# Attention scores with two heads in the two halves of the partitions, ahead of a mixture of experts

## The chip, the cores and the metric

The kernel runs on one core of one Trainium2 chip. The metric is the device time of one execution in microseconds (us); three executions of the kernel before took 622.19, 626.22 and 628.02 us, and their median, 626.22 us, is the time before.

## The reference

Attention over 4 batches of 8 heads, 768 positions, 64 dimensions per head. A query sees the first 4 keys (the sinks) and the 128 keys up to its own position. The result, 3072 tokens of 512 numbers, goes to a mixture of 8 experts that takes one expert per token.

```
scores = scale * np.matmul(q, k.transpose(0, 1, 3, 2))
keep = is_sink | in_window
a = np.exp(np.where(keep, scores, -1e9) - max); a = a / (sum + 1e-09)
x = np.matmul(a, v)                      # rows of 8 heads * 64
logits = xn @ en.T / tau;  expert_idx = argmax(logits)
out[mask] = gate_w[mask, None] * (relu(x[mask] @ w1[e]) @ w2[e])
```

## The kernel before

Everything runs on one core, in two stages: attention with routing, and then the eight experts one after the other. The change lies in the attention alone.

The attention works on 16 pairs of heads (`NP`), each pair in six blocks of 128 queries, in two groups of three blocks (`GROUPS`). For each block, TensorE (PE) computes the scores of both heads into one `sp` tile, which is two banks of PSUM, one per head, 260 columns each: the previous block's keys, the 4 sinks, the current block's keys (`scores`). VectorE (DVE) merges the two blocks by a mask (`merge`) and takes the maximum (`top`), ScalarE (ACT) the exponentials (`exp`). Per group, PE transposes the result, ACT copies it out of PSUM, GpSimd (POOL) cuts it into the parts that belong to each block of values (`sel`), PE multiplies these with the values (`av`) and with the experts' embeddings beside an identity (`xe`), and a DMA stores the rows (`xs<-xr`). There are three `sp` tiles and two further PSUM tiles `w`, which all the other products share.

Ahead of its scores, a pair's queries and keys are split into two parts of 12 bits each, so that fast products (float32r) reach float32 (`prep`). In the kernel before, the host lays every head out twice, in both halves of the 128 partitions. One head has its own loads of q and k (`qn`, `kn`, 128 partitions each) and its own split. The keys end up as `kt`, the first part in partitions 0 to 63 and the second part in 64 to 127: ACT rounds all 128 partitions (line 874), and POOL subtracts in the upper half (line 877). The queries are split by DVE into q1 (line 888) and q2 (line 892), each with the same numbers in both halves; for two heads of all, ACT makes q1. A score block of one head is then two products of 128 rows, q1 and q2 against `kt`, which adds up all four combinations of parts.

The first two pairs (`PLAIN`) are not split: their q and k lie in `raw1` and `raw2`, the staging buffers of the experts' weights, and are multiplied as float32, in one product of 128 rows per head, in which the keys of one head stand beside zeros for the other (line 914). Those buffers are loaded at the very start (`early_loads`, `plain_load`), by the queues of SyncE (SP) and ACT; DVE and POOL write the zeros.

The order on every engine is made ahead of time by a small planner (`Plan`): each piece of work has an engine, a planned duration and a key; among what can start, the smallest key goes first. `KEYS` holds the offsets of the keys by kind of work, `LAST` those of the last pair. Each engine then runs its list strictly in order.

Of the kernel before, what the change touches and what calls it, by code (L numbers as in the profile page):

```python
# [8 lines left out]
F32 = mybir.dt.float32  # L9
# [27 lines left out]
KEYS = dict(sel=-7, ps=1.25, pse=6.25, av=3.75, ote=-42.5, xe=4.25, xee=1.25, k1=7.5, k2=47.25, q1=9.75, q2=0.25, sc=16, mg=-0.25, tp=-0.5, ex=3.25, sk0=-72, sk1=23, tr=-0.75, te=-4.75, rt=2.25, vs=7.75, em=23.25, rc=5.75, lgm=-0.25)  # L37
LAST = dict(mg=9.25, xee=-16.75, tr=-28.25, sc=42.75, ex=31.25, k1=20, sel=7.75, av=35.25, ote=12.5, k2=67, sk1=63.5, rt=52.5, ps=14.75, xe=-2.5, tp=25, q1=25.5, pse=22.75, q2=-0.5, te=60.5, rc=8, lgm=-29.75, vs=63.75, sk0=-31.25, em=-27)
# [17 lines left out]
class Plan:  # L56
    """Orders tasks for engines that issue in order: among those that can start, the one with the smallest key."""
# [22 lines left out]
    def ready(self, t):  # L80
        """when what t waits for is there; None: not known yet"""
# [56 lines left out]
class Kernel:  # L138
# [5 lines left out]
    # ------------------------------------------------------------ constants  # L144
    def constants(self, cp):
# [7 lines left out]
        # run-time scalars: value = (hi + (lo < 0)) * 2^32 + lo, on all partitions  # L153
# [18 lines left out]
    def routing_tiles(self, cp):  # L172
# [17 lines left out]
        # integers on their way to float32  # L190
# [4 lines left out]
    def routing_constants(self):  # L195
        """two parts: GpSimd's, a store"""
        nc = self.nc

        def first():
            nc.gpsimd.memset(self.ones_b[:], 1.0)  # L200
            # tri[k, m] = 1 where k < m
            nc.gpsimd.affine_select(out=self.tri_b[:], in_=self.ones_b[:], pattern=[[1, P]], compare_op=ALU.is_gt, fill=0.0, base=0, channel_multiplier=-1)
            # 8 - e
            nc.gpsimd.iota(self.wi, pattern=[[0, NB], [-1, E]], base=E, channel_multiplier=0)
            # token index of (partition, block), and less NT
            nc.gpsimd.iota(self.tokid[:], pattern=[[P, B * NB]], base=0, channel_multiplier=1)
            nc.gpsimd.iota(self.i3, pattern=[[P, B * NB]], base=-NT, channel_multiplier=1)
            # the free axis, and the slots
# [1131 lines left out]
```

## Time and profile before

| | kernel before |
|---|---|
| median of 3 executions | 626.22 us |
| span of the profiled execution | 620.5 us |
| PE busy | 500.7 us, 81% |
| DVE busy | 367.5 us, 59% |
| ACT busy | 300.5 us, 48% |
| POOL busy | 284.8 us, 46% |
| DMA traffic | 87.45 MB, mean 141 GB/s |

The profile is one further execution with the hardware profiler on; its span runs from the first to the last instruction and leaves out what lies around it. Busy time counts an instruction from its start to its end; products overlap at their ends, so that a busy PE need not be at its peak. A share of the whole span is a mean over two stages that have little in common: the attention ends at about 243 us, and the experts fill the rest.

### The profile page before, as it was taken

Reading aid. Unit: us, or ns where it says so; the run is one execution under the profiler, and the core shown is the slowest. Engines: PE = TensorE matmul, PEld = TensorE weight load, DVE = VectorE, ACT = ScalarE, POOL = GpSimd, SP = SyncE. Lnnn points to the kernel's source line nnn. Section 1 sums busy time; section 2 is a strip of 40 time slices with the busy share of each in tenths; the row PEclk is TensorE's granted clock in tenths of the full one; section 3 lists DMA queues with packets and bytes.
Section 4 is the critical chain, followed back from the end, with each engine's and each line's share of the span. In section 5 each row is a group of like instructions: output and inputs, shape, how many; then the busy total and the mean of one; then the engine's idle time right before and its main releaser. Section 6 shows DMA issues by size and latency. Waiting matters only on the chain.

```text
span 620.5 us, 9493 instructions
## 1 busy us (share of the span) xinstructions
PE 500.7 (81%) x3110; PEld 433.4 (70%) x3110; DVE 367.5 (59%) x728; ACT 300.5 (48%) x847; POOL 284.8 (46%) x420
## 2 busy tenths in 40 slices
PE   0599877898898793599599699888796996999990
PEld 0377666676676672499599488788796995887970
DVE  2488899799989935656356155386372551443510
ACT  0288866786687571355146145145262460351400
POOL 4269886898898843811540610341705203201010
PEclk9989999898999996599899799999797997999996
DMA  3668965665662012542662722542646326221010
GB/s 79 220 237 299 304 206 176 207 188 159 197 213 74 27 52 78 161 142 74 204 200 75 252 74 69 189 161 88 231 137 203 120 70 188 78 73 39 33 39 22
DMA packets 41440, 87.45 MB, mean 141 GB/s; under 512 B 7403, under 2 KB 19691, under 8 KB 41238
## 3 DMA queue, kind: packets, MB, share of 16 engines
q1 hardware_dynamic: 36068, 70.06, 35.7%
q0 software_dynamic: 5040, 14.95, 7.2%
q14 instruction: 155, 1.27, 0.6%
q8 instruction: 47, 0.77, 0.5%
q10 hardware_dynamic: 130, 0.39, 0.2%
HBM read 72.61 MB, written 14.62 MB: 141 GB/s over the span
## 4 chain that ended last, share of the span: by engine, by line
PE 39%; issue 25%; DVE 14%; POOL 7%; DMA 6%; ACT 5%; another core or an unknown queue 1%; SPq 0%; POOLq 0%; DVEq 0%; ACTq 0%
PE h L470 12%; PE y L526 9%; PE y L513 4%; DMA raw<-in_q_dram 3%; PE w L1116 3%; ACT PM L948 2%; DVE mx L937 2%; DVE q L892 2%; DVE sp L927 2%; POOL out_dram L460 2%; PE sp L914 2%; POOL xg L412 1%; POOL kt L877 1%; PE t L442 1%; PE w L1014 1%
## 5 line engine op out<-in xcount | busy, mean ns | idle before, releaser
L470 PE MATMUL h<-xh,W 128*128 128x432 f32 (+7 forms) x512 | 112.9, 367 | 41.4 <-issue 33.7
L470 PEld LDWEIGHTS h<-xh,W 128*128 128x128 f32 x512 | 94.9, 206 | 50.8 <-issue 35.7
L473 DVE SCALAR_TENSOR_TENSOR hl<-h,hh 128x432 fp32r<-128x432 f32 (+7 forms) x64 | 35.9, 561 | 110.5 <-ACT hh L472 52.7
L472 ACT ACTIVATE hh<-h 128x432 fp32r<-128x432 f32 (+7 forms) x64 | 31.7, 496 | 139.1 <-PE h L470 139.1
L380 DVE TENSOR_TENSOR W<-raw,W 128x512 fp32r<-128x512 f32 (+1 forms) x95 | 89.4, 943 | 14.9 <-ACT W L379 14.7
L948 ACT ACTIVATE PM<-sp,mx 128x132 f32<-128x132 f32 (+1 forms) x192 | 69.4, 370 | 34.3 <-DVE mx L937 29.3
L526 PE MATMUL y<-hh,W 128*128 128x432 f32 (+4 forms) x320 | 79.4, 326 | 0.0
L379 ACT CAST W<-raw 128x512 fp32r<-128x512 f32 (+1 forms) x96 | 71.8, 757 | 8.0 <-DVE cnt L365 8.0
L423 POOL TENSOR_TENSOR gn<-gss,half 128x4 f32<-128x4 f32 x8 | 8.3, 1036 | 129.8 <-ACT gjunk L418 129.8
L460 POOL DMA_INDIRECT out_dram<-ys,perm x31 | 30.8, 994 | 64.5 <-DVE ys L514 43.2
L470 PE MATMUL h<-xl,W 128*128 128x432 f32 (+7 forms) x256 | 58.9, 354 | 0.0
L877 POOL TENSOR_TENSOR kt<-kn,kt 64x792 fp32r<-64x792 f32 x28 | 55.7, 1989 | 4.1 <-POOL PM L975 2.1
L526 PEld LDWEIGHTS y<-hh,W 128*128 128x128 f32 x320 | 55.8, 188 | 0.4
L513 PE MATMUL y<-W,hh 128*128 128x512 f32 (+1 forms) x176 | 55.1, 394 | 0.0
L918 PE MATMUL sp<-kt,q 128*128 128x260 f32 x168 | 49.8, 321 | 5.6 <-ACT PM L948 5.4
L408 POOL DMA_INDIRECT xg<-xs,perm x28 | 28.6, 1023 | 52.2 <-PE t L450 29.7
L526 PE MATMUL y<-hl,W 128*128 128x432 f32 (+4 forms) x160 | 51.3, 320 | 0.0
L470 PEld LDWEIGHTS h<-xl,W 128*128 128x128 f32 x256 | 47.2, 201 | 3.2
L1116 PE MATMUL w<-PA,vn 128*64 128x256 f32 (+1 forms) x448 | 47.1, 351 | 2.7 <-POOL PA L1102 2.7
L919 PE MATMUL sp<-kt,q 128*128 128x260 f32 x168 | 43.9, 285 | 0.0
L1116 PEld LDWEIGHTS w<-PA,vn 128*64 128x64 f32 x448 | 29.2, 141 | 19.2 <-issue 5.1
L927 DVE COPY_PREDICATED sp<-mask,sp 128x256 f32<-128x256 int32 x80 | 33.3, 420 | 13.3 <-PE sp L919 5.9
(176 smaller groups left out, 1033.9 us busy)
## 6 DMA issues: line engine op xcount, KB each, us to landing
raw<-in_moe_w_dram SPq DMA_DIRECT2D x64, 512.0 KB, 4.7
kn<-in_k_dram SPq DMA_DIRECT2D x28, 396.0 KB, 4.0
qn<-in_q_dram SPq DMA_DIRECT2D x28, 384.0 KB, 3.7
vn<-in_v_dram SPq DMA_DIRECT2D x16, 384.0 KB, 3.7
xs<-xr SPq DMA_DIRECT2D x16, 384.0 KB, 3.1
raw<-in_k_dram SPq DMA_DIRECT2D x4, 198.0 KB, 14.2
xg<-xs,perm POOLq DMA_INDIRECT x32, 6.3
out_dram<-ys,perm POOLq DMA_INDIRECT x31, 7.1
```

Of the source, the lines that this page charges most:

```text
L379: nc.scalar.copy(w[:, 0, c, s], r)
L380: (eng or nc.vector).tensor_tensor(out=w[:, 1, c, s], in0=r, in1=w[:, 0, c, s].bitcast(F32), op=ALU.subtract)
L460: nc.gpsimd.indirect_dma_start(out=self.outv[4 * e + c], out_offset=Offset(ap=perm[:, e, c : c + 1], axis=0), in_=ysb[:, c, :], in_offset= ...
L470: nc.tensor.matmul(h[:, :N], lhsT=W1[:, l, d, fs], rhs=r[:, d, :N], start=k == 0, stop=k == 3 * NDB - 1)
L513: nc.tensor.matmul(y[0:m, :], lhsT=l[:, f, cs], rhs=W2[:, r, f, :], start=f + j == 0, stop=f + j == NFB + 1)
L526: nc.tensor.matmul(y[:, :N], lhsT=W2[:, l, f, ms], rhs=r[:, f, :N], start=k == 0, stop=k == 3 * NFB - 1)
L877: nc.gpsimd.tensor_tensor(out=kt[D:], in0=kf()[D:], in1=kt[D:].bitcast(F32), op=ALU.subtract)
L918: nc.tensor.matmul(sp[:, h, : KW + P], lhsT=q1[:, js], rhs=rhs, start=True, stop=False)
L919: nc.tensor.matmul(sp[:, h, : KW + P], lhsT=q2[:, js], rhs=rhs, start=False, stop=True)
L927: nc.vector.copy_predicated(sp[:, :, 0:P], self.mask[:], sp[:, :, KW : KW + P])
L948: self.nc.scalar.activation(PM[:, c, h, 0 : hi - lo], sp[:, h, lo:hi], AF.Exp, bias=mx[:, h : h + 1], scale=1.0, accum_out=self.SM[b][:, j ...
L1116: nc.tensor.matmul(o[0][64 * h : 64 * h + 64, (q - a) * P : (q - a + n) * P], lhsT=vt[0][:, h, j, :], rhs=PA[g][0][:, j - lo + 1, h, q - j ...
```

## The change

The two heads of a pair now lie in the two halves of the partitions, on the host too: head 0 in partitions 0 to 63, head 1 in 64 to 127. One load of q and one of k serve the pair, in `prep` as for the first two pairs. The split runs once per pair: ACT rounds the keys into one tile, POOL subtracts the rest into a second tile over all 128 partitions, DVE makes q1 and q2 (ACT makes none). A score block is now three combinations (first by first, first by second, second by first; the product of the two second parts is left out), each as two products of 64 rows, one per head, so that consecutive products alternate between the halves of the array. The first two pairs lose their zeros and take one product of 64 rows per head. The sinks' transposed parts (`pst`) get two buffers instead of one. The planner's durations and all its keys have other values.

```diff
-KEYS = dict(sel=-7, ps=1.25, pse=6.25, av=3.75, ...
+KEYS = dict(sel=-6, ps=0, pse=1, av=-0.5, ...
...
-Q1_ACT = (1, 5)
...
 def plain_load(self, p, i, engines=None):
-        eq.dma_start(q, self.q[2 * p : 2 * p + 2].rearrange("h (r d) s -> (h r) d s", r=2)[0::3])
-        for h in range(2):
-            hs = slice(h * D, (h + 1) * D)
-            ek.dma_start(k[hs, h, P:], self.k[2 * p + h, hs].rearrange("d c s -> d (c s)"))
+        eq.dma_start(q, self.q[p])
+        ek.dma_start(k[:, P:], self.k[p].rearrange("d c s -> d (c s)"))
...
 def prep(self, plan, p):
-        for h in range(2):
-            for tag, shape, src in ((f"kn{h}", [P, NB, KW], self.k[2 * p + h]), (f"qn{h}", [P, S], self.q[2 * p + h])):
+        for tag, shape, src in (("kn", [P, NB, KW], self.k[p]), ("qn", [P, S], self.q[p])):
...
-                nc.gpsimd.tensor_tensor(out=kt[D:], in0=kf()[D:], in1=kt[D:].bitcast(F32), op=ALU.subtract)
+            nc.gpsimd.tensor_tensor(out=kb, in0=kf(), in1=ka.bitcast(F32), op=ALU.subtract)
...
 def scores(self, n):
-            nc.tensor.matmul(sp[:, h, : KW + P], lhsT=q1[:, js], rhs=rhs, start=True, stop=False)
-            nc.tensor.matmul(sp[:, h, : KW + P], lhsT=q2[:, js], rhs=rhs, start=False, stop=True)
+            parts = [(q1, k1), (q1, k2), (q2, k1)]
+        for i, (q, k) in enumerate(parts):
+            for h in range(2):
+                nc.tensor.matmul(sp[:, h, : KW + P], lhsT=q[hs[h], js], rhs=k[hs[h], ks], start=i == 0, stop=i == len(parts) - 1)
...
-                    pst.append(self.pa.tile([32, S], F32R, tag="pst", name="pst", bufs=1))
+                    pst.append(self.pa.tile([32, S], F32R, tag="pst", name="pst", bufs=2))
...
 def early_loads(self, fc):
-            for h in range(2):
-                o = slice((1 - h) * D, (2 - h) * D)
-                eng.memset(k[o, h], 0.0)
-                eng.memset(k[h * D : (h + 1) * D, h, 0:P], 0.0)
+            eng.memset(k[:, 0:P], 0.0)
```

The places where the order on an engine matters below are three. First SP's queue at the start of the program, before (`raw_65` and `raw_66` are the staging buffers of the first and the second pair):

```order
L1250 DMA raw<-in_ints_dram 128x4
L841 DMA raw_65<-in_k_dram 64x792 x2
L838 DMA raw_66<-in_q_dram 128x1x768
L841 DMA raw_66<-in_k_dram 64x792 x2
L1260 DMA tau_t<-in_moe_tau_dram 128x1
L1262 DMA em<-in_moe_expert_emb_dram 8x512
L1267 DMA vraw<-in_v_dram 32x1024
```

The same place in the changed kernel:

```order
L1239 DMA raw<-in_ints_dram 128x4
L838 DMA raw_65<-in_k_dram 128x792
L837 DMA raw_66<-in_q_dram 128x768
L838 DMA raw_66<-in_k_dram 128x792
L1246 DMA tau_t<-in_moe_tau_dram 128x1
L1248 DMA em<-in_moe_expert_emb_dram 8x512
L1253 DMA vraw<-in_v_dram 32x1024
```

The order is the same; four half loads of k became two whole ones, and the load of q has lost its inner dimension of one (the first pair's q, on ACT's queue, in the same way). Second, DVE in the middle of the attention, before (`q_…<-qn` is q1, `q_…<-qn,q` is q2; `sp` and `mx` are masks and maxima of score blocks):

```order
L927 COPY_PREDICATED sp<-mask,sp 128x2x128
L888 TENSOR_SCALAR q_1293<-qn_888 128x768
L937 TENSOR_REDUCE mx<-sp 128x2
L892 SCALAR_TENSOR_TENSOR q_1303<-qn_888,q_1293 128x768
L888 TENSOR_SCALAR q_1318<-qn_944 128x768
L927 COPY_PREDICATED sp<-mask,sp 128x2x128
L892 SCALAR_TENSOR_TENSOR q_1328<-qn_944,q_1318 128x768
L937 TENSOR_REDUCE mx<-sp 128x2
```

And in the changed kernel:

```order
L916 COPY_PREDICATED sp<-mask,sp 128x2x128
L877 TENSOR_SCALAR q_1380<-qn 128x768
L926 TENSOR_REDUCE mx<-sp 128x2
L881 SCALAR_TENSOR_TENSOR q_1398<-qn,q_1380 128x768
L920 COPY_PREDICATED sp<-mask_105,neg 128x2x128
```

Between two masks stood up to two of the four splitting operations of a pair; now a pair has two, of the same shape. Third, PE between two groups, before (`vs` and `vn` are values, `psn` the sinks' part, `kt,q` score products):

```order
L1113 MATMUL w<-pst,vs 128x384
L1116 MATMUL w<-PA,vn 64x256 x4
L1116 MATMUL w<-PA,vn 64x128 x2
L1071 MATMUL w<-ident,psn 32x128 x3
L918 MATMUL sp<-kt_181,q_369 128x260
L919 MATMUL sp<-kt_181,q_391 128x260
L918 MATMUL sp<-kt_182,q_414 128x260
L919 MATMUL sp<-kt_182,q_426 128x260
```

And in the changed kernel:

```order
L1102 MATMUL w<-pst,vs 128x384
L1105 MATMUL w<-PA,vn 64x256 x4
L1105 MATMUL w<-PA,vn 64x128 x2
L1060 MATMUL w<-ident,psn 32x128 x3
L908 MATMUL sp<-kt_171,q_638 128x260 x2
L908 MATMUL sp<-kt_172,q_638 128x260 x2
L908 MATMUL sp<-kt_171,q_656 128x260 x2
```

The neighbours of a score block are the same kinds of work; the block itself went from four products to six, in pairs of which one reads the lower and one the upper half of the partitions.

## Rows read from the trace of the kernel before

**Rows 1.** Busy time by engine in the steady stretch of the attention; header first
```profile
core 0: us, PE busy (x) PEld busy (x) DVE busy (x) ACT busy (x) POOL busy (x), PEclk, DMA share, GB/s
36.00:204.00 168.00, 145.89 (x1145) 115.68 (x1143) 154.02 (x314) 127.91 (x461) 141.22 (x222) 0.98 0.62 197
```
**Rows 2.** Timeline of the start: start us, us, engine, line, work, [idle before <-releaser]
```profile
0.81 1.15 ACTq L838 DMA_DIRECT2D raw<-in_q_dram  x1
2.50 0.66 SPq L838 DMA_DIRECT2D raw<-in_q_dram  x1
...
5.86 0.63 POOL L813 MEMSET kt<- 128x128 f32 x4 [0.85 <-DVE fi L165]
...
18.80 0.56 DVE L849 TENSOR_SCALAR raw<-raw 128x768 f32<-128x768 f32 x1 [13.65 <-DMA raw<-in_q_dram]
...
19.42 5.57 PE L914 MATMUL sp<-raw 128*128 128x260 f32 x12 [19.42 <-DVE raw L849]
...
23.47 0.56 DVE L849 TENSOR_SCALAR raw<-raw 128x768 f32<-128x768 f32 x1 [4.11 <-DMA raw<-in_q_dram]
...
24.70 0.41 DVE L931 COPY_PREDICATED sp<-mask,neg 128x256 f32<-128x256 int32 x1
```
**Rows 3.** Busy time in one microsecond of the start, columns as in rows 1
```profile
14.00:15.00 1.00, 0.00 (x0) 0.00 (x0) 0.00 (x0) 0.00 (x0) 0.00 (x0) 1.00 0.13 49
```
**Rows 4.** DMA issues by work: count, KB each, us from issue to landing
```profile
kn<-in_k_dram SPq DMA_DIRECT2D x28, 396.0 KB, 4.0
qn<-in_q_dram SPq DMA_DIRECT2D x28, 384.0 KB, 3.7
...
raw<-in_k_dram SPq DMA_DIRECT2D x4, 198.0 KB, 14.2
```
**Rows 5.** Groups by line, 36 to 204 us: count | busy us, mean ns | idle before
```profile
L892 DVE SCALAR_TENSOR_TENSOR q<-qn,q 128x768 fp32r<-128x768 f32 x26 | 30.2, 1160 | 0.0
...
L888 DVE TENSOR_SCALAR q<-qn 128x768 fp32r<-128x768 f32 x25 | 19.3, 774 | 0.0
...
L877 POOL TENSOR_TENSOR kt<-kn,kt 64x792 fp32r<-64x792 f32 x26 | 52.0, 1999 | 3.9 <-POOL PM L975 2.1
L1102 POOL TENSOR_SCALAR_AFFINE_SELECT PA<-PT 128x768 f32<-128x768 f32 (+1 forms) x26 | 23.9, 917 | 0.0
...
L874 ACT CAST kt<-kn 128x792 fp32r<-128x792 f32 x27 | 23.1, 856 | 0.0
```
**Rows 6.** One line of DVE, whole run: shortest/median/longest ns
```profile
L929 DVE COPY_PREDICATED sp<-mask,neg x16: 174/175/1803, 25.9 to 215.9; 128x8 f32<-128x8 int32 x16
```
**Rows 7.** Chain that ended last, where it runs through PE: start us, us, what
```profile
39.58 0.88 PE sp L914 x4
...
215.68 1.45 PE w L1116 x16
...
218.04 0.74 PE w L1126 x6
218.78 0.33 PE w L1014 x3
...
220.10 0.37 PE w L1113
220.47 1.23 PE w L1116 x12
...
222.99 0.33 PE w L1071 x3
```
**Rows 8.** Timeline of PE: two score products, and one product group at low clock
```profile
110.61 0.28 PE L919 MATMUL sp<-kt,q 128*128 128x260 f32 x1
110.73 0.28 PE L918 MATMUL sp<-kt,q 128*128 128x260 f32 x1
...
118.06 2.40 PE L1116 MATMUL w<-PA,vn 128*64 128x256 f32 x12
```
**Rows 9.** Waits of PE's weight loads, 36 to 204 us: total us, times, longest
```profile
PEld w L1116 <- issue: 4.2, 21, 0.3
```

More of the change, by code (lines that the diff above doesn't have):

```diff
@@ L809, in fast_attention @@
             self.pss = En(tc.tile_pool(name="a_pss", bufs=self.bufs["sp"], space=PSUM))
-            self.kt = [[one.tile([P, P + NB * KW], F32R, tag=f"kt{i}{h}", name=f"kt{i}{h}") for h in range(2)] for i in range(2)]
+            self.kt = [[one.tile([P, P + NB * KW], F32R, tag=f"kt{i}{c}", name=f"kt{i}{c}") for c in range(2)] for i in range(2)]
             for a in self.kt:
@@ L832, in plain_views @@
         n = P + NB * KW
-        return raw[:, 0 : 2 * n].rearrange("p (h n) -> p h n", h=2), raw[:, 2 * n : 2 * n + S]
+        return raw[:, 0:n], raw[:, n : n + S]
     def plain_load(self, p, i, engines=None):
@@ L901, in q1_act, with f @@
-    def q1_act(self, p, h):
-        return 2 * p + h in Q1_ACT
+        L = []
+        for tag, shape, src in (("kn", [P, NB, KW], self.k[p]), ("qn", [P, S], self.q[p])):
+            b, tile = plan.buf(tag), []
+            def f(tag=tag, shape=shape, src=src, tile=tile):
+                tile.append(ld.tile(shape, F32, tag=tag, name=tag, bufs=2))
+                nc.sync.dma_start(tile[0][:], src)
+            L.append((plan.add("SP", 1.1, NB * p - 9, f, use=[b]), b, tile))
+        (lk, bk, tk), (lq, bq, tq) = L
@@ new lines, in prep, with k1, k2, q1 @@
+        ka, kb = (t[:, P:] for t in self.kt[i])
+        kf = lambda: tk[0][:].rearrange("p c s -> p (c s)")
+        b1, b2, bt = plan.buf("q1"), plan.buf("q2"), plan.buf("kt")
+        t1, t2 = [], []
+        def k1():
+            nc.scalar.copy(ka, kf())
+        def k2():
+            nc.gpsimd.tensor_tensor(out=kb, in0=kf(), in1=ka.bitcast(F32), op=ALU.subtract)
+        def q1():
+            t1.append(ld.tile([P, S], F32R, tag="q1", name="q1"))
+            nc.vector.tensor_scalar(t1[0][:], tq[0][:], 0.125, None, op0=ALU.mult)
@@ new lines, in q2 @@
+        def q2():
+            t2.append(ld.tile([P, S], F32R, tag="q2", name="q2"))
+            nc.vector.scalar_tensor_tensor(out=t2[0][:], in0=tq[0][:], scalar=0.125, in1=t1[0][:].bitcast(F32), op0=ALU.mult, op1=ALU.subtract)
+        K = KEYS
+        a = plan.add("ACT", 0.86, key + K["k1"], k1, [lk], [bk, bt])
+        c = plan.add("POOL", 2.0, key + K["k2"], k2, [a], [bk, bt])
+        d = plan.add("DVE", 0.65, key + K["q1"], q1, [lq], [bq, b1])
+        e = plan.add("DVE", 1.05, key + K["q2"], q2, [d], [bq, b1, b2])
@@ L910, in scores @@
         js, ks = slice(j * P, (j + 1) * P), slice(j * KW, j * KW + KW + P)
-        for h in range(2):
-            if p in PLAIN:
-                k, q = self.plain_views(PLAIN.index(p) % 2)
-                nc.tensor.matmul(sp[:, h, : KW + P], lhsT=q[:, js], rhs=k[:, h, ks], start=True, stop=True)
-                continue
-            q1, q2 = self.Q[p][h][0][0], self.Q[p][h][1][0]
-            rhs = self.kt[self.KT[p]][h][:, ks]
-            nc.tensor.matmul(sp[:, h, : KW + P], lhsT=q1[:, js], rhs=rhs, start=True, stop=False)
-            nc.tensor.matmul(sp[:, h, : KW + P], lhsT=q2[:, js], rhs=rhs, start=False, stop=True)
+        hs = [slice(h * D, (h + 1) * D) for h in range(2)]
+        if p in PLAIN:
+            k, q = self.plain_views(PLAIN.index(p) % 2)
+            parts = [(q, k)]
+        else:
+            q1, q2 = self.Q[p][0][0][0], self.Q[p][0][1][0]
+            k1, k2 = self.kt[self.KT[p]]
+            parts = [(q1, k1), (q1, k2), (q2, k1)]
+        for i, (q, k) in enumerate(parts):
+            for h in range(2):
+                nc.tensor.matmul(sp[:, h, : KW + P], lhsT=q[hs[h], js], rhs=k[hs[h], ks], start=i == 0, stop=i == len(parts) - 1)
     def merge(self, n):
@@ L1004, in sk1 @@
                 nc.gpsimd.tensor_copy(f(3), f(2))
[L1006 removed]
+            sinks.append(plan.add("POOL", 1.15, key + K["sk1"], lambda a=sk0, c=sk1: (a(), c()), xs, [bp, bn]))
             for h in range(2):
```

63 lines of the change are left out of this document (14 added, 49 removed).

## The prediction

> **What bounds the kernel now.** The page's slices show two stages. The experts, from about 243 us on, compute the same in both kernels, so I look at the attention only, and there at three places: the start, the steady stretch, the drain.
>
> *The start* [rows 2]. The timeline shows DVE idle for 13.65 us, then scaling the first pair's q at 18.80 us, because q lands only then; the q of the second pair lands at 23.47 us. DVE runs in order and both scalings come ahead of the first mask, so the first score block is worked on at 24.70 us, although POOL was through the program's first branch at 5.86 us. In between, the one-microsecond row shows a DMA share of 0.13 and 49 GB/s [rows 3]: two of sixteen engines' worth. A load of q of the same size in the steady stretch lands in 3.7 us [rows 4].
>
> *The steady stretch*, 36 to 204 us. POOL's line 1102 runs there 26 times [rows 5], twice per pair, so the stretch holds 13 pairs of 168/13 = 12.9 us. By the busy row [rows 1], DVE works 154.0/13 = 11.85 us per pair, 92%, POOL 10.9, ACT 9.8. DVE is the tightest engine. Part of its time is no work of its own: line 929, eight elements per partition, has a median of 175 ns but runs up to 1803 ns [rows 6], which is the length of POOL's line 877 (1999 ns) [rows 5]; in such cases DVE stands while POOL runs. PE's busy time overlaps at the ends, so I sum its pace from the chain [rows 7] and from the starts of two score products, 0.12 us apart [rows 8]: per pair 6 x 4 x 0.12 = 2.9 (scores), 4 x 0.33 (line 1014), 2 x 0.33 (line 1071), 2 x 0.37 (line 1113), 1.23 + 1.45 (line 1116), 2 x 0.74 (line 1126), together 9.8 us. The engines hold each other up, and a pair takes 12.9/11.85 = 1.09 times the tightest one.
>
> *The drain*, after 204 us, is a chain of PE and DVE work of the last pair that the change reorders but does not shorten; I cost it at nothing, give or take 1 us.
>
> **The change, part by part.**
>
> *First loads.* All four become plain loads of 128 partitions, the shape that lands in 3.7 to 4.0 us [rows 4]. Together they are 2 x 384 + 4 x 198 = 1560 KB; even at the mean of the steady stretch, 197 GB/s [rows 1], that is 8 us from about 2 us on. The lower bound for landing is 2.5 + 3.7 = 6.2 us. DVE needs 1.23 us from the second scaling to the first mask [rows 2], and PE takes 5.57/3 = 1.9 us for its first block, since it begins at half clock: 12 products took 5.57 us there and four take 0.88 us later [rows 2, 7]. I put the first mask at 10.7 us, 14 us earlier. PE had up to three blocks ready at 24.70 us and will have one, which I charge with 1.5 us: **-12.5 us**. At the slow end the loads still need the 14.2 us of the old k loads [rows 4]: 2.5 + 14.2 + 1.2 = 17.9, a gain of 7; at the fast end PE's first block bounds it, a gain of 15. The Trainium skill, "DMA: Bandwidth & Descriptors", section on why a DMA increments its semaphore by 16, says that a DMA runs on as many engines as divide the slowest dimension of both sides; the old q load, two heads outermost, would get two, the new one sixteen. The trace's 0.13 agrees, and by that rule the early landing is all but certain. The smaller memsets lie under the same load wait and are worth nothing by themselves.
>
> *DVE.* q1 and q2 take (30.2 + 19.3)/13 = 3.8 us per pair now [rows 5]; one of each, 0.77 + 1.16, remains: -1.9. The shorter POOL queue should also free DVE of standing: line 929 alone stands for up to 1.8 - 0.2 = 1.6 us at a time [rows 6]; I take 0.5 us per pair, between 0 and 1. DVE: 11.85 - 1.9 - 0.5 = 9.5 us.
>
> *POOL and ACT.* One subtraction of 2.0 us instead of two, over 128 instead of 64 partitions but with the same 792 elements each, so I keep its duration: POOL 10.9 - 2.0 = 8.9. ACT loses one rounding, 0.86 us [rows 5]: 9.0. In loads a pair saves 780 KB; with the DMA share at 0.62 [rows 1] that is worth nothing by itself.
>
> *PE* is the open part: six products of 64 rows instead of four of 128. No row shows two row halves side by side. The nearest row is line 1116, whose products alternate between the halves of the columns: its x12 group is 1280 columns in float32 for the two heads, which at the pace of the undivided float32 product (0.44 us for 260 columns [rows 7]) would be 2.17 us; it took 1.23, so 1.76 times as fast. At that rate six products take 0.72/1.76 = 0.41 us. The bounds are 0.36 (full overlap) and 0.72 (none) per block, against 0.48 now. Then there is the change of form: ahead of line 1116, where the products go from one shape of the array to another, the weight load waits 4.2/21 = 0.2 us for nothing that the profile shows [rows 9]. With one such gap a block costs 0.41 + 0.2 = 0.6, with one on each side and no overlap 1.1 us. The Trainium skill, "TensorEngine Tiling (Array Packing)", section Key Properties, says that a change of tiling mode drains the array while a change of tile does not; by that rule each run of score blocks pays on both sides (a rival below). I take 0.6, because the gap's row is a wait at one side only: PE per pair 9.8 + 6 x (0.6 - 0.48) = 10.5 us.
>
> *Sum.* PE becomes the tightest engine: 10.5 x 1.09 = 11.4 us per pair, against 12.9: 1.5 us for 14 split pairs, **-21 us**. The first two pairs, no longer beside zeros, gain or lose inside the start. 620.5 - 12.5 - 21 = 587 us of span; the median of the executions lies 5.7 us above the profiled span, so I forecast **593 us**. Own range 582 to 606, from a start gain of 7 to 15 and a pair between 10.9 and 11.9 us.
>
> **The rivals.**
>
> *The halves overlap fully and the gap hides.* Then PE is at or under DVE's 9.5: 10.4 us per pair, 2.5 x 14 = 35 less, 579 us. For it: distinct PSUM banks for the two heads. Against: line 1116's 1.76, and three other engines at 9 us, in order.
>
> *The halves do not overlap.* 0.72 per block: PE 11.2, pair 12.3, gain 0.6 x 14 = 9: 605 us. For it: nothing here shows overlap of rows.
>
> *They overlap, but the gap comes on both sides.* 0.41 + 0.4 = 0.8 per block: PE 11.7, pair 12.8, gain 0.1 x 14 = 2: 612 us. For it: score blocks stand between products of other shapes. Against: of two neighbours of line 1116 the waits [rows 9] show one. This is what the drain rule of the Trainium skill's tiling page would make of it.
>
> *The array drains on both sides of every score block, with no overlap: slower.* 1.1 us per block gives PE 13.5, a pair of 14.7, a loss of 1.8 x 14 = 25: 626.2 - 12.5 + 25 = 639 us. It decides from the point at which 14 pairs lose the 12.5 of the start, 13.8 us per pair or 0.97 us per block. For it: both doubts of the last two cases at once. Against: products of several shapes already take turns, and the chain's paces [rows 7] contain their gaps.
>
> *PE's clock falls.* The stretch had 0.98 of 2.4 GHz [rows 1]; at low clock line 1116's group took 2.40 us instead of 1.23 [rows 7, 8]. If half-filled products left the clock at 1.2 GHz for a third of the time, PE would need 10.5 x 1.33 = 14 us and lose as in the last case, some 640 us.
>
> *The start does not move.* Then 593 + 12.5 = 605 us. Against: the loads' shape, above.
>
> **How the numbers follow.** Forecast 0.55; full overlap 0.13; no overlap 0.10; overlap with gaps on both sides 0.07; start unmoved 0.05; drains on both sides 0.06; clock 0.04. The likeliest is 593 us. From 577 to 614 us the range leaves out the two slow cases and the far end of the fast one. A measurement of this kernel tells apart about 1%, 6 us, so faster means under 620 us: the first five cases but a tail, 0.89; the tail and the milder ends of the slow cases, 0.05, stay within 1%; slower 0.06.
>
> **What would show it.** First scaling of q before 9 us and the first mask near 11 us (start); the raw loads of q and k landing in 4 to 7 us; rows from one store of `xr` to the next near 11.4 us; DVE at 80 to 85% of the steady stretch with two splitting operations per pair; line 929's counterpart with fewer long runs; the six products of a score block starting within 0.6 us, two and two nearly together, and the granted clock at 0.95 or more. If the six starts lie 0.12 us apart, PE's term is wrong and the time goes to 605; if weight loads wait on both sides of each block, to 620 and above.

## The result, and the profile after

The changed kernel takes **597.68 us** (median of four executions, 592.88 to 600.27) against 625.73 us for the kernel before, measured together with it: a ratio of **0.9583** with a 95% interval of 0.9535 to 0.9632, so 4.2% faster. Between the two medians lie 28 us, a ratio of 0.9552, which is inside the interval; the ratio itself stands for 26 us. The forecast was 593 us, its range 577 to 614. The profiled execution of after is its longest, 600.27 us with a span of 598.5. Runs that were not measured together are compared below by their ratios to the kernel before; 0.01 is 6.2 us. The row of e10 in the table below is read from one of its two slow executions (617.45 us, where its ratio rests on the other two, 608.05 and 614.97 us).

The start in the timeline of after, in the columns of [rows 2]:

```profile
7.28 1.45 POOL L812 MEMSET kt<- 128x128 f32 x4 [4.31 <-DVE fi L164]
7.33 1.13 DVE L846 TENSOR_SCALAR raw<-raw 128x768 f32<-128x768 f32 x2 [0.76 <-DVE fi L164]
7.96 2.97 PE L908 MATMUL sp<-raw 64*128 64x260 f32 x12 [7.96 <-DVE raw L846]
...
9.84 0.41 DVE L920 COPY_PREDICATED sp<-mask,neg 128x256 f32<-128x256 int32 x1
```

The DMA issues of the first loads in after, in the columns of [rows 4]:

```profile
raw<-in_k_dram SPq DMA_DIRECT2D x2, 396.0 KB, 5.6
raw<-in_q_dram ACTq DMA_DIRECT2D x1, 384.0 KB, 5.0
raw<-in_q_dram SPq DMA_DIRECT2D x1, 384.0 KB, 6.1
```

The first mask comes at 9.84 us instead of 24.70 [rows 2], and DVE now waits for the program's first branch (`fi`), no longer for a load.

For the steady stretch I take the first product on the sinks' values, of which each pair has two. Its row gives count, shortest/median/longest ns, and the starts of the first and the last of them: 26 of these products are 25 steps, or 12.5 pairs. Before:

```profile
L1113 PE MATMUL w<-pst,vs x26: 433/438/684, 62.7 to 224.5; 32*128 32x384 f32 x26
```

After, the same row:

```profile
L1102 PE MATMUL w<-pst,vs x26: 433/437/683, 43.1 to 201.7; 32*128 32x384 f32 x26
```

The busy time in the same stretch, before, in the columns of [rows 1]:

```profile
62.40:224.80 162.40, 137.82 (x1087) 109.03 (x1084) 147.19 (x303) 118.60 (x437) 134.64 (x216) 0.98 0.55 169
```

And after:

```profile
42.80:202.00 159.20, 150.62 (x1266) 107.61 (x1264) 123.60 (x288) 114.17 (x435) 103.23 (x207) 0.95 0.38 112
```

The splitting by line in this stretch of after (columns of [rows 5]):

```profile
L881 DVE SCALAR_TENSOR_TENSOR q<-qn,q 128x768 fp32r<-128x768 f32 x12 | 16.5, 1372 | 0.0
...
L877 DVE TENSOR_SCALAR q<-qn 128x768 fp32r<-128x768 f32 x11 | 6.9, 624 | 0.0
...
L873 POOL TENSOR_TENSOR kt<-kn,kt 128x792 fp32r<-128x792 f32 x12 | 26.4, 2199 | 1.2 <-ACT kt L870 1.2
```

And the row of after that answers to [rows 6]:

```profile
L918 DVE COPY_PREDICATED sp<-mask,neg x16: 174/225/985, 11.1 to 196.2; 128x8 f32<-128x8 int32 x16
```

A pair took (224.5 - 62.7)/12.5 = 12.94 us and takes 12.69. PE is busy for 95% of the stretch where DVE was at 91%. Half of the splitting work of [rows 5] is gone, yet the pair is only 0.25 us shorter. In the same way for every run (busy us per pair are shares of the stretch times the pair; clock is the mean granted clock there):

| kernel | ratio, 95% interval | pair | PE | DVE | ACT | POOL | clock |
|---|---|---|---|---|---|---|---|
| before | 1 | 12.94 | 10.98 | 11.73 | 9.45 | 10.73 | 0.98 |
| after | 0.9583 (0.9535-0.9632) | 12.69 | 12.00 | 9.85 | 9.10 | 8.23 | 0.95 |
| e1 before, plain first loads of q | 0.9779 (0.9731-0.9828) | 12.92 | 11.07 | 11.73 | 9.47 | 10.78 | 0.97 |
| e2 heads in turn | 0.9621 (0.9577-0.9664) | 12.72 | 12.05 | 9.82 | 9.10 | 8.21 | 0.95 |
| e3 q split twice | 0.9998 (0.9964-1.0032) | 14.04 | 12.17 | 11.49 | 9.14 | 9.12 | 0.95 |
| e4 old keys | 0.9552 (0.9505-0.9600) | 11.86 | 11.20 | 9.40 | 9.03 | 8.03 | 1.00 |
| e5 e4, four products | 0.9414 (0.9374-0.9455) | 11.51 | 10.70 | 9.29 | 9.02 | 8.13 | 1.00 |
| e6 e4, three products | 0.9434 (0.9395-0.9473) | 11.46 | 10.38 | 9.39 | 8.97 | 8.16 | 0.99 |
| e7 e4, q1 on ACT | 0.9439 (0.9373-0.9505) | 11.66 | 11.22 | 8.47 | 9.61 | 8.06 | 0.99 |
| e8 e4, long runs | 0.9683 (0.9637-0.9730) | 12.51 | 11.52 | 9.07 | 8.86 | 8.06 | 0.95 |
| e9 after, pauses filled | 0.9576 (0.9504-0.9648) | 12.27 | 11.82 | 9.97 | 9.10 | 8.23 | 0.99 |
| e10 e4, POOL twice | 0.9791 (0.9691-0.9891) | 13.53 | 11.98 | 10.69 | 9.13 | 9.67 | 0.94 |
| e11 e4, q1 half on ACT | 0.9625 (0.9555-0.9695) | 12.58 | 11.62 | 9.40 | 9.54 | 8.18 | 0.99 |
| e12 e5, q split twice | 0.9887 (0.9836-0.9938) | 13.53 | 11.71 | 10.72 | 9.15 | 8.90 | 0.93 |

### The profile page after: what moved, and what is told of

The parts are those of the page before. It is cut to its first block, busy times and chain, and to the rows that moved or that the text cites. A ratio compares the mean times of both kernels' runs of the same rounds, so it can differ in the third digit from the quotient of the medians.

```text
span 598.5 us, 9677 instructions
## 1 busy us (share of the span) xinstructions
PE 506.5 (85%) x3278; PEld 422.5 (71%) x3278; DVE 338.0 (56%) x698; ACT 291.9 (49%) x832; POOL 246.8 (41%) x403
## 4 chain that ended last, share of the span: by engine, by line
PE 53%; issue 25%; DVE 8%; POOL 6%; ACT 3%; DMA 1%; another core or an unknown queue 1%; POOLq 0%; DVEq 0%; ACTq 0%
PE h L469 14%; PE y L525 10%; PE w L1105 6%; PE sp L908 6%; PE w L1115 4%; PE y L512 4%; PE w L1003 3%; PE w L1060 2%; POOL out_dram L459 2%; POOL xg L411 2%; PE w L1102 2%; PE t L441 1%; ACT PM L937 1%; DVE sp L920 1%; DVE q L881 1%
## 5 line engine op out<-in xcount | busy, mean ns | idle before, releaser
L379 DVE TENSOR_TENSOR W<-raw,W 128x512 fp32r<-128x512 f32 (+1 forms) x95 | 90.9, 959 | 14.9 <-ACT W L378 14.7
L937 ACT ACTIVATE PM<-sp,mx 128x132 f32<-128x132 f32 (+1 forms) x192 | 68.8, 367 | 16.5 <-DVE mx L926 11.0
L908 PE MATMUL sp<-kt,q 64*128 64x260 f32 x504 | 50.7, 316 | 1.0 <-ACT PM L937 1.0
L1105 PE MATMUL w<-PA,vn 128*64 128x256 f32 (+1 forms) x448 | 49.1, 362 | 0.0
L908 PEld LDWEIGHTS sp<-kt,q 64*128 64x128 f32 x504 | 35.6, 191 | 14.3 <-issue 6.9
L926 DVE TENSOR_REDUCE mx<-sp 128x2 f32<-128x264 f32 (+1 forms) x96 | 40.6, 425 | 2.2
```

The lines of the kernel that those rows point to most:

```text
L379: (eng or nc.vector).tensor_tensor(out=w[:, 1, c, s], in0=r, in1=w[:, 0, c, s].bitcast(F32), op=ALU.subtract)
L908: nc.tensor.matmul(sp[:, h, : KW + P], lhsT=q[hs[h], js], rhs=k[hs[h], ks], start=i == 0, stop=i == len(parts) - 1)
L926: self.nc.vector.tensor_reduce(out=mx[:], in_=self.SP[n][:, :, lo:hi], axis=AX.X, op=ALU.max, negate=True)
L937: self.nc.scalar.activation(PM[:, c, h, 0 : hi - lo], sp[:, h, lo:hi], AF.Exp, bias=mx[:, h : h + 1], scale=1.0, accum_out=self.SM[b][:, j ...
L1105: nc.tensor.matmul(o[0][64 * h : 64 * h + 64, (q - a) * P : (q - a + n) * P], lhsT=vt[0][:, h, j, :], rhs=PA[g][0][:, j - lo + 1, h, q - j ...
```

## The experiments

### The change taken apart: e1, e5, e4

e1 is the kernel before with only the loads of q of the first two pairs changed, each to one plain load of 64 partitions per head:

```diff
-        eq.dma_start(q, self.q[2 * p : 2 * p + 2].rearrange("h (r d) s -> (h r) d s", r=2)[0::3])
+        for h in range(2):
+            hs = slice(h * D, (h + 1) * D)
+            eq.dma_start(q[hs], self.q[2 * p + h, hs])
```


> The kernel before, with one edit: the first two pairs' q are loaded by two plain loads of 64 partitions each, instead of one load whose outer dimension is two heads. Theory (the start is worth its whole time, since nothing later takes it up): first mask near 10 to 12 us instead of 24.7, and 12 to 15 us less, 611 to 614 us, about half of the whole gain of 28. Rival (the first loads are late but the stretch after them, bound by DVE, catches up or waits elsewhere): the first mask comes early and the time falls by less than 6 us.

Measured: 608.75 us, 0.9779, so **-13.8 us** from the form of these two loads alone. Its timeline:

```profile
6.88 0.75 DVE L851 TENSOR_SCALAR raw<-raw 128x768 f32<-128x768 f32 x1 [1.53 <-DMA raw<-in_q_dram]
...
9.44 0.59 DVE L851 TENSOR_SCALAR raw<-raw 128x768 f32<-128x768 f32 x1 [1.81 <-DMA raw<-in_q_dram]
...
10.69 0.41 DVE L933 COPY_PREDICATED sp<-mask,neg 128x256 f32<-128x256 int32 x1
```

The mask comes 14.0 us earlier and 13.8 of them reach the end, as the theory had it. One microsecond of e1 while these loads run, in the columns of [rows 3]:

```profile
5.00:6.00 1.00, 0.00 (x0) 0.00 (x0) 0.31 (x2) 0.00 (x0) 0.01 (x1) 1.00 1.01 228
```

The Trainium skill, "DMA: Bandwidth & Descriptors", section on why a DMA increments its semaphore by 16, has a load run on as many engines, up to 16, as divide its slowest dimension; the traces agree: the share of 0.13, two of sixteen, with the dimension of two heads [rows 3] is 1.01, all sixteen, without it.

e4 is the changed kernel with the tables `KEYS` and `LAST` of before:

```diff
-KEYS = dict(sel=-6, ps=0, pse=1, av=-0.5, ...
+KEYS = dict(sel=-7, ps=1.25, pse=6.25, av=3.75, ...
...
```


> The changed kernel with the planner's keys of the kernel before (KEYS and LAST); layout, loads and products stay. Theory (layout and loads bring the gain, the keys little): 597 to 606 us. Rival (the steady stretch's 9 us come from the new keys): 607 us or more.

e5 is e4 with the four products of 128 rows of the kernel before; the order on all engines is that of e4. In the new layout such products add the scores of the two heads, so e5, and e6 and e12 below, leave out the parting of the heads and serve the measurement only. Their tokens go to the experts a little differently: in e5 and e12 two experts have products of 320 and 416 columns instead of 336 and 400, the same in sum.

```diff
-        for i, (q, k) in enumerate(parts):
...
             for h in range(2):
-                nc.tensor.matmul(sp[:, h, : KW + P], lhsT=q[hs[h], js], rhs=k[hs[h], ks], ...)
...
+        for h in range(2):
+            for i in (0, 2):
+                nc.tensor.matmul(sp[:, h, : KW + P], lhsT=parts[i][0][:, js], rhs=parts[i][1][:, ks], ...)
```


> The changed kernel with the table of numbers of before (595.43 us, 11.86 us per pair of heads in the steady stretch), but each score block of a split pair made of the four products of 128 rows of the kernel before instead of six of 64 rows; the scores of the two heads are thereby added together, which is the part of the computation that this kernel changes. Everything else, loads, splits and the order on every engine, stays. This measures what the new form of the products costs by itself. Theory A: six products of 64 rows cost no more by their pace (0.46 us a block against 0.48), but the change of form ahead of them makes the weight load wait, 6.0 us in 181, or 0.47 us per pair; then a pair falls to 11.5 us and the time to about 590. Rival: the waits at the change of form lie beside other engines' work; the time stays within 593 to 598.

Measured: e4 595.43 us (0.9552), a little under the range of its theory, so that its rival fell; e5 586.42 us (0.9414). Starts of the sinks' products in e4:

```profile
L1102 PE MATMUL w<-pst,vs x26: 433/438/442, 46.7 to 195.0; 32*128 32x384 f32 x26
```

and in e5:

```profile
L1106 PE MATMUL w<-pst,vs x26: 433/438/441, 46.0 to 189.9; 32*128 32x384 f32 x26
```

The busy row of e4, columns of [rows 1]:

```profile
46.40:195.30 148.90, 140.52 (x1247) 101.18 (x1245) 118.00 (x282) 113.32 (x434) 100.80 (x208) 1.00 0.38 114
```

and that of e5:

```profile
45.70:190.20 144.50, 134.26 (x1097) 108.38 (x1097) 116.64 (x282) 113.19 (x435) 102.06 (x208) 1.00 0.39 116
```

So the change has four parts, each a difference of ratios at 623 us. Beside them stands the same difference in the attention alone, read in one execution of each kernel from the start of the cast of the routing counts, which ends the attention; before, e1, e5, e4 and after:

```profile
L359 DVE CAST cnt<-w x1: 155/155/155, 242.6 to 242.6; 128x8 int32<-128x8 f32 x1
L359 DVE CAST cnt<-w x1: 156/156/156, 226.1 to 226.1; 128x8 int32<-128x8 f32 x1
L358 DVE CAST cnt<-w x1: 156/156/156, 207.1 to 207.1; 128x8 int32<-128x8 f32 x1
L358 DVE CAST cnt<-w x1: 156/156/156, 212.2 to 212.2; 128x8 int32<-128x8 f32 x1
L358 DVE CAST cnt<-w x1: 155/155/155, 218.9 to 218.9; 128x8 int32<-128x8 f32 x1
```

| part | by the ratios, us | attention in the profiles, us |
|---|---|---|
| the start (e1) | **-13.8** | -16.5 |
| less work on DVE, POOL and ACT (e1 to e5) | **-22.7** | -19.0 |
| six products of 64 rows (e5 to e4) | **+8.6** | +5.1 |
| the new keys (e4 to after) | +1.9 | +6.7 |
| sum | -26.0 | -23.7 |

The intervals put 3 to 4 us on each number of the first column, and the second leaves out the experts, which take 377.7 to 382.5 us in these five profiles. So the new form of the products costs 5 to 9 us, and the new keys cannot be told from nothing by the ratio, though the attention is 6.7 us longer with them; e2 below, with the same keys, ends its attention at 219.3 us. The second part is not pure either: between e1 and e5 the planner makes another order, the two plain pairs lose their zeros and `pst` has a second buffer, and none of these was measured apart. Theory A of e5 held for the pair, 11.51 us, and the new form costs TensorE 0.50 us per pair by its busy time.

What a block costs is seen in the timeline of after: the first two, four and six score products of a run, all twelve of its two blocks with the work behind them, and the weight loads ahead of them with their wait.

```profile
107.02 0.39 PE L908 MATMUL sp<-kt,q 64*128 64x260 f32 x2
...
107.02 0.51 PE L908 MATMUL sp<-kt,q 64*128 64x260 f32 x4
...
107.02 0.63 PE L908 MATMUL sp<-kt,q 64*128 64x260 f32 x6
...
107.02 0.99 PE L908 MATMUL sp<-kt,q 64*128 64x260 f32 x12
107.94 0.88 PE L1003 MATMUL w<-ident,PM 128*128 128x128 f32 x6
...
107.02 0.54 PEld L908 LDWEIGHTS sp<-kt,q 64*128 64x128 f32 x8 [0.21 <-issue]
```

The waits of these weight loads in after, 42.8 to 202 us, in the columns of [rows 9]:

```profile
PEld sp L908 <- issue: 6.5, 33, 0.4
```

The same two blocks in the timeline of e5: the first of eight products of 128 rows, all eight, and the work behind them:

```profile
106.78 0.37 PE L912 MATMUL sp<-kt,q 128*128 128x260 f32 x1
...
106.78 1.21 PE L912 MATMUL sp<-kt,q 128*128 128x260 f32 x8
107.83 0.90 PE L1119 MATMUL w<-IE,oT 128*128 128x144 f32 x6
```

Two products of 64 rows, one per head, add 0.12 us together, as much as one of 128 rows [rows 8]: the halves overlap fully, 3 x 0.12 = 0.36 us a block. From the first start to the next work the two blocks take 0.92 us instead of 1.05. What is lost is lost at the ends of a run: at the entry the weight load waits 0.2 us, 33 times; at the exit, with 0.28 us for the last product, 0.21 us lie between its start and the next work (107.73 to 107.94), against 0.12 in e5 (107.71 to 107.83). That the first two products of a run take 0.39 us instead of 0.28 is no cost of the new form, since the first product takes 0.37 us in e5 too. The Trainium skill, "TensorEngine Tiling (Array Packing)", section Key Properties, says that a change of mode drains the array; the wait agrees with it, at this price.

### Does the alternation matter: e2

```diff
-        for i, (q, k) in enumerate(parts):
-            for h in range(2):
+        for h in range(2):
+            for i, (q, k) in enumerate(parts):
```


> The changed kernel, with the six products of a score block in another order: the three of head 0, then the three of head 1, so that neighbours share a half of the rows. Theory (alternation lets two row halves run side by side, and PE sets the pace of the attention): starts 0.12 us apart instead of 0.077, a block 0.72 instead of 0.46 us, 84 blocks x 0.26 = 22 us more, 616 to 622 us. Rival (products of 64 rows are shorter by themselves, or PE does not set the pace): 595 to 602 us.

Measured: 599.51 us, 0.9621; my theory fell, the rival held. The group of twelve products at the same place (two blocks, timeline of PE in e2) and the work behind it:

```profile
107.19 1.00 PE L908 MATMUL sp<-kt,q 64*128 64x260 f32 x12
108.11 0.33 PE L1003 MATMUL w<-ident,PM 128*128 128x128 f32 x1
```

Twelve products took 0.92 us from start to start of the next work in both, 107.02 to 107.94 in after and 107.19 to 108.11 here. Three products of one half in a row do not keep the other half from working beside them.

### Is PE the bound now: e6, e3, e12, e10

e6 is e4 with three products of 128 rows, the least TensorE work here:

```diff
...
+        for h, i, start, stop in ((0, 0, True, False), (1, 1, True, True), (0, 2, False, True)):
+            nc.tensor.matmul(sp[:, h, : KW + P], lhsT=parts[i][0][:, js], rhs=parts[i][1][:, ks], start=start, stop=stop)
```


> As the run with four products, but with three products of 128 rows per block, one for each term of the split (the scores of the two heads are added together and split over the two banks, which is the part of the computation that this kernel changes). TensorE's time for a block falls from 0.46 to 0.36 us, and no form changes: 0.6 + 0.47 = 1.07 us less per pair. Theory A: TensorE sets the pace, a pair falls by about 1 us to 10.8 and the time by 15 to 580. Theory B: the engines work in a chain, each a part of the pair's time, with VectorE at 9.6 us and ScalarE at 9.1 close behind; then half or less of it comes back, 587 to 592.

Measured: 588.49 us, 0.9434, no better than e5 although PE has 0.3 us less per pair. Its theory B holds: from e5 on, TensorE's time is not what is short.

e3 is the changed kernel with both splits of q done a second time on DVE; e12 is e5 with the same addition:

```diff
             nc.vector.tensor_scalar(t1[0][:], tq[0][:], 0.125, None, op0=ALU.mult)
+            s = ld.tile([P, S], F32R, tag="s1", name="s1")
+            nc.vector.tensor_scalar(s[:], tq[0][:], 0.125, None, op0=ALU.mult)
...
+            nc.vector.scalar_tensor_tensor(out=s[:], in0=tq[0][:], scalar=0.125, in1=t1[0][:].bitcast(F32), op0=ALU.mult, op1=ALU.subtract)
```


> The changed kernel, with q1 and q2 of each pair computed a second time into tiles that nobody reads: DVE gets back the 1.9 us per pair that the change took from it, in the same order of work. Theory (PE sets the pace now, and the relief of DVE went into its waits for score products, 30 us): 0 to 7 us more, 597 to 605 us. Rival (DVE still sets the pace, or all engines together do): 14 x 1.9 = 27 us more, at least 18, so 615 to 625 us.

> The run with four products of 128 rows per block (586.42 us, 11.51 us per pair; the scores of the two heads are added together, which is the part of the computation that it changes), with both splits of q done a second time on VectorE in every split pair, 2.0 us more, as much as the change took away there. TensorE, ScalarE, GpSimd and the order on all engines stay as in that run, so that the relief of VectorE is taken back and that of ScalarE, GpSimd and the transfers kept. VectorE then has 9.2 + 2.0 = 11.2 us per pair. Theory A, the forecast's rule (a pair takes 1.09 times the tightest engine): 12.2 us per pair, 14 x 0.7 = 10 more, 596 us. Theory B, each engine's time adds to the chain at nearly its full length, as with the six products of 64 rows (24 us for the same addition): 14 x 1.4 to 1.7 = 20 to 24 more, 606 to 611 us; then the whole relief of the change was VectorE's.

Measured: e3 621.39 us, 0.9998, +26 us by the ratios, so that PE alone does not set the pace and the rival held; e12 617.27 us, 0.9887, +29 us over e5. The busy row of the same 12.5 pairs in e3:

```profile
45.60:221.70 176.10, 152.63 (x1266) 108.43 (x1264) 144.10 (x313) 114.64 (x435) 114.40 (x207) 0.95 0.33 101
```

and in e12:

```profile
50.90:220.60 169.70, 146.87 (x1096) 114.68 (x1094) 134.53 (x303) 114.75 (x434) 111.69 (x207) 0.93 0.32 98
```

In e12 no engine is busy for more than 87%, DVE for 79%, and the pair is 13.53 us, longer than before the change. Both theories of e12 fell, A by far; B, too, left out that the granted clock would drop from 1.00 to 0.93. The planner does not know of the added work, so its order may no longer fit; how much of the 29 us is order, clock or DVE's own time stays open.

e10 is e4 with POOL's subtraction done twice:

```diff
             nc.gpsimd.tensor_tensor(out=kb, in0=kf(), in1=ka.bitcast(F32), op=ALU.subtract)
+            nc.gpsimd.tensor_tensor(out=kb, in0=kf(), in1=ka.bitcast(F32), op=ALU.subtract)
```


> The changed kernel with the table of numbers of before (595.43 us), GpSimd's subtraction of a pair's keys done a second time in all 14 split pairs: GpSimd has 2.2 us more per pair, 10.3 instead of 8.1, under VectorE's 9.6 and TensorE's 11. Theory A, GpSimd has slack and only makes others late where they wait for it: up to 5 us more, 595 to 601. Theory B, VectorE stands while GpSimd works, as the step on line 929 in the forecast had it: VectorE's time per pair grows by 0.5 us or more and the time by 8 to 25 us, 603 to 620; the forecast's 0.5 us per pair for one subtraction less is then right or too small.

Measured: 0.9791, which is 611 us beside the kernel before of that measurement, +15 us over e4; theory B. DVE's work is that of e4, but its busy time per pair grows from 9.40 to 10.69 us in the profiled executions. The group of the second split of q shows where, in e4 (columns of [rows 5]):

```profile
L881 DVE SCALAR_TENSOR_TENSOR q<-qn,q 128x768 fp32r<-128x768 f32 x11 | 15.8, 1441 | 0.0
```

and in e10:

```profile
L882 DVE SCALAR_TENSOR_TENSOR q<-qn,q 128x768 fp32r<-128x768 f32 x11 | 22.8, 2075 | 0.0
```

How the two engines meet is seen in the timeline of after, where the subtraction of keys (POOL) and the second split of q (DVE) start close together twice:

```profile
64.19 1.04 DVE L881 SCALAR_TENSOR_TENSOR q<-qn,q 128x768 fp32r<-128x768 f32 x1
64.39 2.56 POOL L873 TENSOR_TENSOR kt<-kn,kt 128x792 fp32r<-128x792 f32 x1
...
76.72 1.87 POOL L873 TENSOR_TENSOR kt<-kn,kt 128x792 fp32r<-128x792 f32 x1 [0.42 <-ACT kt L870]
77.01 2.40 DVE L881 SCALAR_TENSOR_TENSOR q<-qn,q 128x768 fp32r<-128x768 f32 x1
```

The one that starts first keeps its usual time, and the other takes longer by about what is left of it. The two overlap seven times in this stretch of after: in three POOL started first and DVE took 2.28 to 2.40 us, in four DVE started first and POOL took 2.56 to 2.57 us. In e4 they overlap three times, always with POOL first; in e10 POOL is first, and DVE held up, seven times in eleven. So what a pair loses on DVE depends on which of the two the order starts first.

The Trainium skill, "SBUF — State Buffer", section SBUF: two separate sides, has VectorE with two SBUF inputs and GpSimd hold a shared port for a whole instruction; these times agree, and so do the 0.63 us more of one instruction on the mean in e10, with nothing changed but POOL.

### What the clock has to do with it: e9

After has the clock at half (1.2 of 2.4 GHz) four times in the stretch, each time within 1.4 us of the end of a pause of PE. The pauses come to 1.4, 1.9, 1.4 and 1.4 us, the first two each in two pieces. Those four windows in the columns of [rows 1]:

```profile
60.80:67.60 6.80, 6.80 (x38) 4.31 (x38) 2.43 (x5) 4.25 (x15) 4.77 (x7) 0.50 0.05 9
84.70:88.10 3.40, 3.40 (x18) 1.56 (x18) 2.38 (x8) 1.14 (x5) 0.51 (x1) 0.51 0.06 23
132.50:135.90 3.40, 3.40 (x20) 2.57 (x18) 2.81 (x12) 1.82 (x9) 1.56 (x3) 0.50 0.59 212
159.80:163.20 3.40, 3.40 (x21) 2.19 (x18) 0.27 (x1) 1.67 (x6) 0.57 (x3) 0.51 0.38 115
```

Ahead of the second and the third, PE waits for DVE in the routing of a batch; the waits of PE from 78 to 85 and from 126 to 133 us in after:

```profile
PE w L1060 <- DVE rk L299: 1.2, 1, 1.2
PE w L291 <- DVE oh L283: 0.7, 1, 0.7
...
PE w L291 <- DVE oh L283: 1.4, 1, 1.4
```

e9 fills these two pauses:

```diff
             st["R"] = R = w[:, 0 : m * E].rearrange("p (b e) -> p b e", b=m)
+            for i in range(24):
+                nc.tensor.matmul(w[:, 384:512], lhsT=self.tri_b[:], rhs=self.ones_b[:], start=True, stop=True)
```


> The changed kernel, whose granted clock falls to half four times in the steady stretch (from 60.8, 84.7, 132.5 and 159.8 us, 17 us in all), each time after a pause of TensorE of 1.2 to 1.5 us within some 4 us. Two of the four pauses, at 81 and 130 us, are waits for VectorE in the routing of a batch (lines 283 and 299). Here 24 products of 128 columns on constants, which nobody reads, are put ahead of the product that waits there, so that TensorE works through the pause. Theory A, the clock falls because TensorE paused: the falls at 84.7 and 132.5 us vanish, 6.8 us at half clock become full ones, and from the first to the last product on the values of the sinks the kernel takes 185 us instead of 188.4, the whole 594 to 596 us. Rival: the falls stay or move, the stretch takes 188 to 190 us, the whole 597 to 600.

Measured: the filled pause in the timeline of e9, its products at work where PE waited:

```profile
80.34 1.17 PE L292 MATMUL w<-ones_b,tri_b 128*128 128x128 bf16 x18
```

The second, the third and the fourth place in e9, columns of [rows 1]:

```profile
84.70:88.10 3.40, 3.40 (x34) 2.40 (x30) 2.29 (x9) 2.52 (x10) 0.81 (x4) 1.00 0.03 7
132.50:135.90 3.40, 3.40 (x33) 2.72 (x31) 3.32 (x12) 1.68 (x7) 0.53 (x3) 1.00 0.02 8
155.60:159.00 3.40, 3.40 (x21) 2.17 (x17) 0.27 (x1) 1.65 (x6) 0.55 (x3) 0.50 0.38 114
```

And the starts of the sinks' products in e9:

```profile
L1104 PE MATMUL w<-pst,vs x26: 433/437/441, 44.3 to 197.7; 32*128 32x384 f32 x26
```

The two filled falls are gone, the unfilled fourth stays; the first, whose pause shrank from 1.4 to 0.8 us, is gone too. 12.5 pairs take 153.4 us instead of 158.6, with more work on PE. So theory A holds for the attention. In the whole, 599.61 us (0.9576), which is where the rival put it, the gain cannot be seen: the routing counts came 3 us earlier, at 215.9 us, but the experts behind them took 384.8 us in this profile and 379.6 in that of after, with the same instructions. Over the profiles of all runs they take 377.5 to 384.8 us, which hides a gain of 3 us.

### Attempts at a better version: e7, e8, e11

e7 is e4 with the first part of q made by ACT, e11 the same in every second split pair (`act = p % 2 == 0`):

```diff
-            nc.vector.tensor_scalar(t1[0][:], tq[0][:], 0.125, None, op0=ALU.mult)
+            nc.scalar.mul(t1[0][:], tq[0][:], 0.125)
...
-        d = plan.add("DVE", 0.65, key + K["q1"], q1, [lq], [bq, b1])
+        d = plan.add("ACT", 0.86, key + K["q1"], q1, [lq], [bq, b1])
```

e8 is e4 with a planner that goes on with score blocks on PE once it is at one:

```diff
...
-                t = min((x for x in c if x[0] <= t0 + 0.1), key=lambda x: (x[1].key, x[1].i))
+                c = [x for x in c if x[0] <= t0 + 0.1] + [x for x in c if x[1].sc and self.in_sc and t0 + 0.1 < x[0] <= t0 + 0.3]
+                t = min(c, key=lambda x: (not (x[1].sc and self.in_sc), x[1].key, x[1].i))
...
```

In all three the planner makes another order.

> The changed kernel with the table of numbers of before (595.43 us), and the first part of q made by ScalarE instead of VectorE in all 14 split pairs: VectorE 0.65 us less per pair, ScalarE 0.86 us more, TensorE the same. Theory A, TensorE alone sets the pace: 593 to 598. Theory B, every microsecond of VectorE counts (a doubled split, 2.0 us per pair, cost 24 us over 14 pairs, 0.86 us per us): 0.65 x 0.86 x 14 = 8 less, about 587, less whatever ScalarE's 9.1 + 0.9 = 10 us then cost.

> As the run with the first part of q on ScalarE (588.72 us), but in every second split pair only: VectorE 9.2 and ScalarE 9.5 us per pair on the mean, nearer to each other than 8.8 and 10. Theory B (each engine's time counts, in a chain): about the same, 586 to 591, or a little less if the slower of the two counts most, 584 to 587. Rival: only VectorE's relief counts, then half the gain is lost, 591 to 593.

> The changed kernel with the table of numbers of before (595.43 us), and a planner that goes on with score blocks on TensorE when it is at one: 49 runs of score products instead of 63, so 14 changes into the form of 64 rows and 14 out of it fewer, at 0.2 us or a little more each way. Theory A (TensorE's changes of form count): 3 to 6 us less, 590 to 592. Rival: what TensorE saves is lost where the blocks come in bunches and the other engines wait for the work pushed back: 595 or more.

Measured: e7 588.72 us (0.9439), as theory B had it, and the fastest version here that leaves nothing out: its interval, 0.9373 to 0.9505, ends below those of both after and before; e11 601.94 us (0.9625), outside all three expectations; e8 604.61 us (0.9683), the rival. e11 has less work on DVE than e4, though the same busy time (9.40 us per pair), and less load on ACT than e7, and is slower than both. e8 does the work of e4 in another order and takes 8 us more by the ratios. So the order itself moves 5 to 10 us, and that e7's gain is DVE's relief is not shown.

## Why the prediction was right, and where not

The sign and the two sources of the gain (an early start, then DVE relieved and PE next) were right, and 597.68 lies within both ranges. The start came out as forecast; of the 21 us of the steady stretch 12.2 came by the ratios, and that the sum ended only 4.7 us off is in part luck. Step by step:

- **Start.** Forecast -12.5, measured -13.8 (e1). The loads land in 5.0 to 6.1 us as foreseen; DVE's first mask is at 9.84 (10.7 forecast; 10.69 in e1).
- **DVE, POOL, ACT.** Forecast 9.5, 8.9 and 9.0 us per pair; 9.40, 8.03 and 9.03 in e4, 9.85, 8.23 and 9.10 in after. Standing behind POOL was named rightly, but it moved: line 918 runs up to 0.99 us instead of 1.80 [rows 6], while the mean of the second split, now one per pair, is 1372 ns instead of 1160 [rows 5].
- **PE.** 0.6 us a block was forecast as partial overlap (0.41) and a gap of 0.2 for every block. Overlap is full (0.36); the gap of 0.2 comes once per run of one or two blocks, and some 0.1 us more at its end, so that the rival with gaps on both sides was right in part. In sum the block is near the forecast: 0.12 us more were foreseen, 0.50/6 = 0.08 came by PE's busy time. The 0.12 should have cost 0.12 x 6 x 1.09 x 14 = 11 us; it cost 8.6 by the ratios, 5.1 in the attention of the profiles.
- **The step that failed** is "a pair takes 1.09 times the tightest engine". It was read from a kernel in which DVE alone was at 92%. e5 keeps PE's old work, 9.8 us by the paces, and has DVE at 9.3: the rule gives 10.7 us, measured 11.51 (1.17 times). With PE's new work, 10.5 as forecast, it gives 11.4: 11.86 in e4 (1.13 times), and 12.69 in after. So of the 1.29 us by which a pair of after is longer than forecast, 0.46 come with the ratio and 0.83 with the new keys, in whose order the clock falls; e9, with three of the four falls gone, gives 0.42 of them back. A likely reason for the larger ratio is that engines that issue in order and hand each other three `sp` tiles wait more when several are nearly alike; no run here changes the tiles, so this is not shown. Everything behind the start was to bring -21 us and brought -22.7 + 8.6 + 1.9 = -12.2 by the ratios, 7.2 from e1 to after in the attention of the profiles.
- **The new keys** stand in the change, and the forecast put them at nothing without a reason. By the ratios they are worth nothing that can be told, in the profiles they lengthen the attention by 6.7 us.
- **The clock.** Taken as unchanged; the rival had it low for a third of the time. That rival's 10.5 x 1.33 is a third of the work at half clock; a third of the time would be 10.5 x 1.2 = 12.6, a pair of 13.7 and some 625 us instead of 640. In the profile of after the clock was low for 17 of 159 us, half of which is 8.5 us of TensorE's work, where PE is at 95%. It was low for a third as long as the rival had it, but 8.5 us is as much as the steady stretch missed; 5.2 us of it came back in e9.
- **Luck.** The forecast took 33.5 us off; the ratio stands for 26.0, 7.5 less: 1.3 more at the start, 8.8 less behind it. The number 593 is yet only 4.7 off, because it is held against a median, and the medians of a few executions lie 28 us apart where the ratio stands for 26. The 5.7 us between span and median are 1.7 by which an execution's time exceeds its span (622.19 and 620.5) and 4.0 by which the median lay above that shortest execution; in after the median lies 4.8 above the shortest, so that this term did no harm.

## What to carry to other kernels

Relief of the tightest engine is worth its length only down to the next engines, and where three of them are within some 15% of each other, the pair took longer than the ratio of the old kernel has it, here 1.13 to 1.17 times the tightest instead of 1.09, and more where falls of TensorE's clock followed its pauses. To learn what each part of a change is worth, put one part back under the same order of work: a run with another order differed by 5 to 10 us here for that reason alone. Read the end of the stage in question too, and not only the total: the experts behind the attention vary by 7 us from one profile to the next, which hides a part worth 3 to 7. Look for loads with a tiny outermost dimension first: one line gave half of the gain here.

## What the runs showed of the hardware that was not expected

- Products in the two row halves of the array run fully side by side, 0.12 us for two as for one of 128 rows, also when three of one half are issued ahead of three of the other (e2). The Trainium skill, "TensorE: Matmul & The Clock Gate", Part 3: Packing small matmuls, has products overlap in different row groups and start and end strictly in the order of the program; by the second, e2 would have been slower, and it was not.
- Going over to products of 64 rows costs a wait of 0.2 us of the weight load, and leaving them some 0.1 us (0.21 us from the last product's start to the next work, 0.12 behind products of 128 rows in e5).
- Stretches of 3.4 to 6.8 us at half clock followed pauses of TensorE of 1.4 to 1.9 us, in one piece or two, and filling two such pauses took the falls behind them away (e9). Not every pause has one: PE waits 1.8 us at once in e4, where the clock stays at 1.00.
- Of a VectorE instruction (1.04 us) and a subtraction on GpSimd (1.87 us) that overlap, the one that starts first keeps its time and the other takes 2.40 and 2.56 us (after); one more such subtraction per pair made the VectorE instruction 0.63 us longer on the mean (e10).
